# Result quarters in buffers of their own, the global rows' stores on two queues, and their first product earlier in line

## The chip, the cores and the metric

The kernel runs on one core of a Trainium2 chip. The metric is the device time of one execution in microseconds (us), median of the runs. The core has five engines that run their own instruction streams in order and wait for each other by semaphores: PE (TensorE, matrix products; PEld is its weight load), DVE (VectorE), ACT (ScalarE), POOL (GpSimd) and SP (SyncE, which here only issues transfers). In the profile an engine's name with a q (SPq, DVEq) is its sequencer: issuing a DMA and waiting stand there.

## The reference

```python
# attention: B, H, Sl, Sg, D = 8, 8, 512, 32, 64; keys and values are [global; local]
s_g = scale * q_g @ k_all.T                       # 32 global rows see all 544
out_g = softmax(s_g) @ v_all
s_l = scale * [q_l @ k_g.T, masked(q_l @ k_l.T)]  # 512 local rows see 32 global rows and a band of +-32
out_l = softmax(s_l) @ [v_g; v_l]
x = [out_g; out_l] of every batch, heads side by side: (8 * 544, 512)
# feed-forward
h = x @ w_in                                      # 512 -> 2048
g = h * clip(h + 3, 0, 6) / 6
out = g @ w_out                                   # 2048 -> 512, float32, (4352, 512)
```

## The kernel before, in words

All work is done for one batch after another. For each batch b the attention of four groups of 128 local rows and of the 32 global rows is worked out, its result is turned into `xt[b % 3]`, and then the feed-forward of the 512 local rows follows (`ffn_local`). The global rows of all eight batches, 8 x 32 = 256 rows, are gathered in `xg` and go through the feed-forward together at the very end (`ffn_global`); in the code that is "batch 8".

**First product** ("M1", `first`, L1000): for each of 16 chunks c of the 2048 hidden columns PE multiplies four times (L1007) into one PSUM bank, ACT makes the clipped factor (L1013, tile `t1`), and DVE multiplies the two (L1017) into `gl`, which frees the bank. For local rows a multiplication is 512 columns wide, for the global rows 256.

**Second product.** Batches 6, 7 and 8 (`SEVEN`, L998) do it by a scheme with seven products instead of eight. `sevenths` (L1082) has DVE or POOL add and subtract chunks of `gl` into `vs` (L1070); `pair` (L1099) then multiplies, for 256 rows at a time, seven times, each a run of 8 multiplications 128x256 (`product`, L1123), named by m = 0 to 6 here. Sums of these products are kept in two float32 scratch tiles `ub` (in `xt` and `qT`, taken in turn by the pairs; a pair copies its first product there, L1175, and adds to it, `plus`, L1134). Each pair ends in four quarters of its result, 128 rows x 256 columns: `outs` (L1138) has DVE add a bank and a scratch tile into a staging buffer (L1147), and SP stores that buffer to the output. Batch 6 has two pairs, batch 7 two and batch 8 (the global rows) one, so there are 20 quarters.

**Staging and stores.** Before the change the staging buffer is one of three `ot` tiles (`NOT`, L315), shared with the other batches' results. A quarter takes one (`take=("ot",)`) and the store gives it back, so DVE must not write it again until the store from it has landed. A local quarter is one store of 128 rows x 1 KB (L1214). The rows of a global quarter lie in four batches, so it is four stores of 32 rows (L1240). All are issued by SP, one after another.

**Order of work.** The order on every engine is not written out by hand: each operation is entered with an estimated cost, its predecessors and a rank (`Plan.add`), `Plan.run` plays it through with these costs, and the engines get the order that results (L1373). `pick` (L1326) chooses PE's next operation; among the feed-forward's it takes the one with the lowest `key` (L1288). A batch has 32 pieces of key (`PIECES`); for the global rows M1 had the keys 256 + 0 to 15, and the second product 256 + 16 and up. Batch 7's second product has keys 256 + 1 and up (two per product), so the global rows' M1 and batch 7's second product are interleaved.

With these, PE's order from the first global M1 on is, before the change (P7.0 and P7.1 are the two pairs of batch 7, P8 that of batch 8; in brackets m):

```
7 M1, P7.0[1], 1 M1, P7.0[2], 1 M1, P7.0[3], 2 M1, P7.0[4], 2 M1, P7.0[5], 2 M1, P7.0[6], 1 M1,
P7.1[0], P8[0], P7.1[1], P8[1], P7.1[2], P8[2], P7.1[3], P8[3],
P7.1[4], P8[4], P7.1[5], P8[5], P7.1[6], P8[6]
```

Of the kernel before, what the change touches and what calls it, by code (L numbers as in the profile page):

```python
# [10 lines left out]
FP32 = mybir.dt.float32  # L11
# [228 lines left out]
def kernel(  # L240
# [12 lines left out]
    nc = tc.nc  # L253
    P = 128

    B, H, Sl, D = q_l.shape
    Sg = q_g.shape[2]
# [3 lines left out]
    NJ = Sl // P  # L261
    NU = Sl // Sg
    UJ = P // Sg
    NDFF = dff // P
# [33 lines left out]
    vn = sbs("vn", 2, [P, NJ + 1, H, D1])  # L298
# [14 lines left out]
    NT1 = 4  # L313
    t1 = sbs("t1", NT1, [P, Sl], FP32)
    NOT = 3  # L315
# [13 lines left out]
    NM = 3  # L329
# [4 lines left out]

    plan = Plan()
    add = plan.add
    plan.free = {"m": NM, "t": 2, "s": 4, "a": 4, "t1": NT1, "ot": NOT}
    slots = {"m": list(range(NM)), "t1": list(range(NT1)), "ot": list(range(NOT))}

    def dma(rows, run):  # L340

# [719 lines left out]
    wt = [t.rearrange("p (c f) -> p c f", c=NH) for t in wt]  # L1061
    ut = [t.bitcast(FP32) for t in (xt[(B - 3) % 3].rearrange("p n c -> p (n c)"), qT[0].rearrange("d j p q -> d (j p q)"))]
    wt_op = [None] * 4
    u_use = {}

    def both(dst, a, b, op, n, engines, deps, rank, what):
# [32 lines left out]
    def pair(b, i, n, g, s_, sums, gates, store, banks):  # L1099
        a1, a2 = slice(i * P, (i + 1) * P), slice(n + i * P, n + (i + 1) * P)  # L1100
        left, right = slice(0, HALF), slice(HALF, dm)
        lo, hi = range(NH), range(NH, NDFF)
        k = u_use.setdefault("n", 0) % 2
        u_use["n"] += 1
        ub = [ut[k][:, e * HALF:(e + 1) * HALF] for e in range(4)]
        st = {}
        g1, g2 = [gates[c] for c in lo], [gates[c] for c in hi]

        where = ({"X": (0, left), "W": (0, right), "Y": (1, left), "V": (1, right)} if banks == 2 else
                 {x: (y, left) for y, x in enumerate("XYWV")})  # L1110
        two = banks == 2

        def at(x):
            return pm[st[where[x][0]]][:, where[x][1]]

        prev = [None]

        def product(m, x, lhs, rhs, deps, take=None):
            def emit():
                if take is not None:  # L1120
                    st[take] = slots["m"].pop(0)
                for c in range(NH):
                    nc.tensor.matmul(out=at(x), lhsT=lhs(c), rhs=rhs(c), start=c == 0, stop=c == NH - 1)  # L1123
            prev[0] = add("PE", (NH * (HALF / 2.4 + 2.6), NH), emit, [prev[0]] + deps, (b, 2 * i, m * 8 / 7.0),
                          take=("m",) if take is not None else (), what="M2" if take is not None else "M2+")
            return prev[0]

        def freed(x):
            if x is not None:
                slots["m"].append(st[x])  # L1130

        def plus(dst, a, x, deps, bank=None):
            def emit():
                nc.vector.tensor_tensor(out=dst, in0=a(), in1=at(x), op=ALU.add)  # L1134
                freed(bank)
            return add("DVE", 410.0, emit, deps, (-2.5,), give=("m",) if bank is not None else (), what="sevenths")

        def outs(row, cols, x, a, deps, bank):  # L1138

            so = {}  # L1140
            give = ("m",) if bank is not None else ()
            op = add("DVE", 400.0, None, deps, (-2.4,), take=("ot",), give=give, what="out")

            def emit():
                so["o"] = slots["ot"].pop(0)
                dst = ot[so["o"]][:, 0:HALF]
                nc.vector.tensor_tensor(out=dst, in0=a, in1=at(x), op=ALU.add)  # L1147
                freed(bank)
            op.emit = emit

            def emit_store():
                store(i, row, cols, ot[so["o"]])
                slots["ot"].append(so["o"])
            add("SP", (660.0, P * 62.0 / 16, 62.0, P), emit_store, [op], (b, 2 * i, 9), DMA_LAT, give=("ot",), what="store")
            return op

        def gt(c0, cols):
            return lambda c: g[:, c0 + c, cols]

        def wo_(c0, cols):  # L1160
            return lambda c: w_out[:, c0 + c, cols]

        def su(k_):
            return lambda c: s_[:, k_, c, a1]

        def wt_(k_):
            return lambda c: wt[k_][:, c, :]

        used = u_use.get(k, [])
        p1 = product(0, "X", gt(0, a1), wo_(0, left), g1 + wo, 0)  # L1170
        cx = add(("ACT", "DVE"), (act(HALF), dve(HALF)), None, [p1] + used + m1_done[B - 3] + [s_op[B - 2][j] for j in range(NJ + 2)], (-2.5,), lat=220.0, what="sevenths")

        def copy_x():
            if cx.on == "ACT":
                nc.scalar.copy(out=ub[0], in_=at("X"))  # L1175
            else:
                nc.vector.tensor_copy(out=ub[0], in_=at("X"))
        cx.emit = copy_x
        p6 = product(1, "Y", su(1), wt_(1), sums[1] + [wt_op[1]], 1)
        u2 = plus(ub[1], lambda: ub[0], "Y", [p6, cx], None if two else 1)  # L1180
        p7 = product(2, "W", su(2), wt_(2), sums[2] + [wt_op[2]] + ([cx] if two else []), None if two else 2)
        u3 = plus(ub[2], lambda: ub[1], "W", [p7, u2])
        p5 = product(3, "V", su(0), wt_(0), sums[0] + [wt_op[0]] + ([u2] if two else []), None if two else 3)
        u4 = plus(ub[3], lambda: ub[1], "V", [p5, u2])
        c22 = outs(1, right, "V", ub[2], [p5, u3], None)
        p2 = product(4, "X", gt(NH, a1), wo_(NH, left), g2 + [cx] + ([u3] if two else []))
        c11 = outs(0, left, "X", ub[0], [p2], None if two else 0)
        p3 = product(5, "V", su(3), wo_(NH, right), sums[3] + [c22, u4])
        c12 = outs(0, right, "V", ub[3], [p3, u4], 1 if two else 3)
        p4 = product(6, "W", gt(NH, a2), wt_(3), [u3, wt_op[3]] + ([c11] if two else []))  # L1190
        c21 = outs(1, left, "W", ub[2], [p4], 0 if two else 2)
        u_use[k] = [c11, c12, c21, c22]
        m2_done[b].append(p4)

    def ffn_local(b):
        x = xt[b % 3]
        r = b % 2
        parts = ((0, 2), (2, 4)) if b == 0 else ((0, 4),)
        gates = {}
        for part, (j0, j1) in enumerate(parts):  # L1200
            t0, n = j0 * P, (j1 - j0) * P
            for c in range(NDFF):
                free = m2_done[b - 2] if b >= 2 else vperm[0] + vperm[1] if b == 1 else []
                deps = x_op[b][j0:j1] + wi[c // (NDFF // 4)]

                place = 2 * (c % NH) + c // NH if b in SEVEN else c
                pe, ga = first(lambda m, t0=t0, n=n: x[:, m, t0:t0 + n], n, g_l[r][c][:, t0:t0 + n], c, deps,
                               (b, part, place), "M1", free)
                m1_done[b].append(pe)
                gates[part, c] = ga  # L1210
        if b in SEVEN:
            def quarter(i, row, cols, o):
                r0 = b * S + Sg + (2 * row + i) * P
                nc.sync.dma_start(out=out[r0:r0 + P, cols], in_=o[:, 0:HALF])  # L1214
            sevenths(b, g_all[r], Sl // 2, [gates[0, c] for c in range(NDFF)], vs[r], [], quarter, SEVEN[b])
            return
        for j in range(NJ):
            row = b * S + Sg + j * P
            part = next(k for k, (j0, j1) in enumerate(parts) if j0 <= j < j1)


            half = dm // 2
            for i, cols in enumerate((slice(0, half), slice(half, dm)) if (b, j) == (B - 1, NJ - 1) else (slice(0, dm),)):
                def store(o, row=row, cols=cols):
                    nc.sync.dma_start(out=out[row:row + P, cols], in_=o[:, 0:cols.stop - cols.start])
                m2_done[b].append(second(g_l[r], j * P, [gates[part, c] for c in range(NDFF)], (b, j + i), store, "M2", cols))

    def ffn_global():
# [6 lines left out]
        per = P // Sg  # L1235
        rows = out.rearrange("(b s) d -> b s d", s=S)
        if B in SEVEN:
            def quarter(i, row, cols, o):
                for a in range(per):
                    nc.sync.dma_start(out=rows[row * per + a, 0:Sg, cols], in_=o[a * Sg:(a + 1) * Sg, 0:HALF])  # L1240
            sevenths(B, g_all[B % 2], B * Sg // 2, gates, vs[B % 2], m2_done[B - 2], quarter, SEVEN[B])
            return
        for i in range(B // per):
# [35 lines left out]
    EARLY = 40000  # L1279
    KEYS = (47, 44, -23, 52, 0)  # L1280
    REST = 0

    SOONER = (0, 0, 0, 0, 0, 0, 0, 0)
    KEYED, GLAST = 0, 0
# [3 lines left out]
    def key(op):  # L1288
        if op.key is None:
# [2 lines left out]
                op.key = -1e9  # L1292
            elif r[0] == B:

                op.key = B * PIECES + (r[2] if w == "M1" else NDFF + 4 * r[1] + r[2])
            elif w == "M1":
                op.key = r[0] * PIECES + 2.0 * (r[2] + r[1] * 0.5)
            elif w[0] == "M":
# [109 lines left out]
```

## Time and profile before

| | |
|---|---|
| three runs | 331.44, 332.47, 332.88 us; median 332.47 |
| the profiled execution | 332.08 us |
| its span, first to last instruction | 330.3 us, so 1.78 us lie around the span |
| granted TensorE clock | 0.998 of full speed |

A page of the profile gives busy times by engine; the timeline gives each instruction's start and duration, counted from the span's start, with the idle time before it and what ended that; the view of one source line gives the spread of its durations; the chain of waits goes back from the last instruction to what released each step. A store has two times: its issue on the queue of the engine that issues it (SPq rows), and its landing after that, which the view of the line gives as "DMA to landing".

### The profile page before, as it was taken

The page shows a single profiled execution, that of the slowest core. Times are in us where ns is not written, and L with a number is a line of the kernel's source. Part 1 is how long each engine was busy: PE and PEld are TensorE (multiplying, and loading weights), DVE is VectorE, ACT ScalarE, POOL GpSimd, SP SyncE. Part 2 cuts the span into 40 slices and gives each one's busy share as a digit, 9 for nine tenths or more (in the row PEclk, how much of TensorE's full clock was granted, in tenths as well). Part 3 has the DMA queues.
Part 4 walks back from the last instruction along what each step waited for, and adds up shares of the span by engine and source line. Part 5 has one row for each costly group of instructions (what it writes and reads, how often), then busy time and mean ns, then how long its engine had stood idle before and what let it go on. Part 6 is the DMA issues. An engine that isn't in the chain of part 4 may idle for free.

```text
span 330.3 us, 12995 instructions
## 1 busy us (share of the span) xinstructions
PE 313.9 (95%) x5176; PEld 175.0 (53%) x5176; DVE 264.4 (80%) x1038; ACT 226.8 (69%) x553; POOL 225.4 (68%) x322
## 2 busy tenths in 40 slices
PE   7999888999999899999999999998999999999991
PEld 3446666555444445454445444444444456668881
DVE  3799998677987589959985987599978988879742
ACT  4699998779986797489967966657668645335400
POOL 8487544797399959979978998799970640646300
PEclk9999999999999999999999999999999999999999
DMA  8999999998399999699979998993067512210213
GB/s 129 223 202 188 195 237 194 146 151 186 45 151 182 182 189 115 113 147 147 184 125 146 150 133 156 133 169 81 16 151 118 116 36 69 72 33 33 66 34 93
DMA packets 101212, 43.24 MB, mean 131 GB/s; under 512 B 75968, under 2 KB 98080, under 8 KB 101152
## 3 DMA queue, kind: packets, MB, share of 16 engines
q0 software_dynamic: 45840, 17.47, 47.4%
q1 hardware_dynamic: 55312, 24.95, 38.5%
q8 instruction: 40, 0.66, 0.9%
q14 instruction: 20, 0.16, 0.2%
HBM read 35.13 MB, written 8.91 MB: 133 GB/s over the span
## 4 chain that ended last, share of the span: by engine, by line
PE 71%; DVE 18%; issue 4%; DMA 2%; ACT 2%; SPq 1%; POOL 1%; DVEq 0%; ACTq 0%; POOLq 0%
PE m L1033 22%; PE m L1007 22%; DVE gl L1017 5%; PE m L1123 4%; DVE vs L647 4%; DVE sm L833 3%; PE a L864 3%; PE t L1007 3%; PE s L821 3%; DMA kn<-in_k_l_dram 2%; PE s L1007 2%; PE s L1123 2%; PE t L850 1%; ACT t L1013 1%; PE t L1033 1%
## 5 line engine op out<-in xcount | busy, mean ns | idle before, releaser
L647 POOL COPY vs<-vn 32x528 f16<-32x528 f16 (+1 forms) x186 | 115.8, 622 | 19.3 <-ACT vn L383 5.2
L1007 PE MATMUL m<-xt,win 128*128 128x512 f16 (+1 forms) x496 | 105.1, 352 | 2.6 <-DVE gl L1017 2.4
L837 ACT ACTIVATE ex<-sm,mx 128x128 f16<-128x128 f32 x256 | 85.2, 397 | 19.1 <-DVE mx L833 18.4
L1033 PE MATMUL m<-wout,gl 128*128 128x512 f16 x368 | 90.5, 380 | 0.2 <-DVE gl L1017 0.2
L1017 DVE SCALAR_TENSOR_TENSOR gl<-t,m 128x512 f16<-128x512 f32 (+1 forms) x130 | 76.8, 604 | 16.0 <-ACT t L1013 14.6
L1013 ACT ACTIVATE t<-m 128x512 f32<-128x512 f32 (+1 forms) x130 | 68.5, 539 | 30.5 <-PE m L1007 27.2
L1007 PEld LDWEIGHTS <-win 128*128 128x128 f16 x640 | 59.6, 98 | 51.1 <-issue 4.1
L833 DVE CUSTOM_DVE_ANT_0 sm<-s,mask 128x128 f32<-128x128 f32 x256 | 59.7, 285 | 12.4 <-PE s L821 11.2
L1033 PEld LDWEIGHTS <-gl 128*128 128x128 f16 x384 | 34.5, 98 | 38.5 <-issue 0.6
L1070 POOL TENSOR_TENSOR vs<-gl 128x512 f16<-128x512 f16 (+1 forms) x12 | 12.0, 998 | 33.6 <-DVE gl L1017 24.2
L878 DVE TENSOR_TENSOR x<-a,rec 128x256 f16<-128x256 f32 x64 | 24.0, 417 | 0.1
L355 POOL DMA_DIRECT2D vn<-in_v_l_dram x24 | 21.1, 882 | 1.2 <-DMA kn<-in_k_l_dram 0.8
L833 DVE DVE_READ_ACCUMULATOR2_ANT mx<- 128x1 f32 x256 | 21.3, 83 | 0.0
L821 PE MATMUL s<-kT,qT 64*32 64x128 f16 x1024 | 14.2, 219 | 3.6 <-issue 2.0
L1123 PEld LDWEIGHTS <-vs 128*128 128x128 f16 x160 | 15.7, 98 | 3.5
L821 PEld LDWEIGHTS <-qT 64*32 64x32 f16 x1024 | 8.1, 91 | 14.9 <-issue 14.4
L355 POOL DMA_DIRECT2D vn<-in_v_g_dram x7 | 4.1, 584 | 17.4 <-PE a L967 16.9
L383 ACT COPY et<-t 128x1024 f16<-128x1024 f16 (+1 forms) x13 | 12.8, 987 | 4.5 <-PE t L850 4.5
L864 PEld LDWEIGHTS <-et 128*32 128x32 f16 x1024 | 10.1, 96 | 10.3 <-issue 8.1
L647 DVE COPY vs<-vn 64x528 f16<-64x528 f16 (+1 forms) x24 | 14.2, 591 | 0.6
L864 PE MATMUL a<-vs,et 128*32 128x65 f16 x1024 | 14.3, 195 | 0.2 <-DVE vs L647 0.2
L1007 PE MATMUL t<-xt,win 128*128 128x512 f16 x56 | 14.4, 379 | 0.0
(160 smaller groups left out, 436.7 us busy)
## 6 DMA issues: line engine op xcount, KB each, us to landing
out_dram<-ot SPq DMA_DIRECT2D x24, 256.0 KB, 3.6
qn<-in_q_l_dram POOLq DMA_DIRECT2D x16, 256.0 KB, 5.6
kn<-in_k_l_dram POOLq DMA_DIRECT2D x16, 256.0 KB, 6.9
vs<-vn SPq DMA_DIRECT2D x14, 264.0 KB, 5.9
vn<-in_v_l_dram POOLq DMA_DIRECT2D x24, 128.0 KB, 5.2
win<-in_moe_w_in_dram POOLq DMA_DIRECT2D x4, 512.0 KB, 9.1
wout<-in_moe_w_out_dram POOLq DMA_DIRECT2D x8, 256.0 KB, 9.4
out_dram<-ot SPq DMA_DIRECT2D x16, 128.0 KB, 1.7
```

Of the source, the lines that this page charges most:

```text
L355: op = add("POOL", dma(rows, run), lambda: nc.gpsimd.dma_start(out=dst, in_=src), deps, rank, LOAD_LAT + (MARGIN if what[0] in "vqkg" and ...
L647: (nc.vector if o.on == "DVE" else nc.gpsimd).tensor_copy(out=dst, in_=src)
L821: nc.tensor.matmul(out=pss[e][u * Sg:(u + 1) * Sg, p * P:(p + 1) * P], lhsT=qT[r][rows, j, p, u * Sg:(u + 1) * Sg], rhs=kT[r][rows, p, k0: ...
L833: nc.vector.tensor_tensor_reduce(out=sm[i3][h], in0=pss[e][:, p * P:(p + 1) * P], in1=m, scale=-scale, scalar=3.0e38, op0=ALU.add, op1=ALU ...
L837: nc.scalar.activation(out=ex[ie][:, h, :], in_=sm[i3][h], func=EXP, scale=-1.0, bias=mx[i3][h])
L864: nc.tensor.matmul(out=psa[h // 4][q, c0:c0 + D + 1], lhsT=et[k][:, h * P + u * Sg:h * P + (u + 1) * Sg], rhs=vs[r][:, j * UJ + u, h, 0:D ...
L878: nc.vector.tensor_tensor(out=xs[ix][:, 4 * c * D:4 * (c + 1) * D].rearrange("q (h d) -> q h d", d=D), in0=acc[c][:, :, 0:D], in1=rr[c].to ...
L1007: nc.tensor.matmul(out=ps[:, 0:n], lhsT=w_in[:, m, c * P:(c + 1) * P], rhs=x(m), start=(m == 0), stop=(m == NP - 1))
L1013: nc.scalar.activation(out=t1[st["t"]][:, 0:n], in_=pm[st["m"]][:, 0:n], func=RELU, bias=0.5, scale=1.0 / 6.0)
L1017: nc.vector.scalar_tensor_tensor(out=g, in0=t1[st["t"]][:, 0:n], scalar=1.0, in1=pm[st["m"]][:, 0:n], op0=ALU.min, op1=ALU.mult)
L1033: nc.tensor.matmul(out=pm[st["m"]][:, 0:n], lhsT=g[c][:, t0:t0 + P], rhs=w_out[:, c, cols], start=(c == 0), stop=(c == NDFF - 1))
L1123: nc.tensor.matmul(out=at(x), lhsT=lhs(c), rhs=rhs(c), start=c == 0, stop=c == NH - 1)
```

## The change

- The quarters of batches 6, 7 and 8 get five staging buffers of their own (`oq`), which lie in `vn[0]`, the value tile of the even batches. A quarter therefore also waits for the attention of batch 6, which last reads that tile.
- Of a global quarter's four stores, ACT's queue issues the first two and SP's the last two.
- The planner's costs of a store are other numbers.
- The keys of the global rows' M1 go up by 0.5 instead of 1, and those of their second product begin at 12 instead of 16 (`GLOBALS`).

```diff
-    plan.free = {"m": NM, "t": 2, "s": 4, "a": 4, "t1": NT1, "ot": NOT}
-    slots = {"m": list(range(NM)), "t1": list(range(NT1)), "ot": list(range(NOT))}
+    plan.free = {"m": NM, "t": 2, "s": 4, "a": 4, "t1": NT1, "ot": NOT, "oq": 5}
+    slots = {"m": list(range(NM)), "t1": list(range(NT1)), "ot": list(range(NOT)), "oq": list(range(5))}
...
+    oq = vn[0].rearrange("p n h d -> p (n h d)")[:, 0:10 * HALF].bitcast(FP32).rearrange("p (k c) -> p k c", k=5)
...
-            op = add("DVE", 400.0, None, deps, (-2.4,), take=("ot",), give=give, what="out")
+            op = add("DVE", 400.0, None, deps + [av_op[B - 2][j] for j in range(NJ + 1)] + strips[B - 2], (-2.4,), take=("oq",), give=give, what="out")
 
             def emit():
-                so["o"] = slots["ot"].pop(0)
-                dst = ot[so["o"]][:, 0:HALF]
+                so["o"] = slots["oq"].pop(0)
+                dst = oq[:, so["o"], :]
                 nc.vector.tensor_tensor(out=dst, in0=a, in1=at(x), op=ALU.add)
                 freed(bank)
             op.emit = emit
 
+            half = [add("ACT", 900.0, lambda: store(i, row, cols, oq[:, so["o"], :], nc.scalar), [op], (-1,), lat=0.0, what="store")] if b == B else []
+
             def emit_store():
-                store(i, row, cols, ot[so["o"]])
-                slots["ot"].append(so["o"])
-            add("SP", (660.0, P * 62.0 / 16, 62.0, P), emit_store, [op], (b, 2 * i, 9), DMA_LAT, give=("ot",), what="store")
+                store(i, row, cols, oq[:, so["o"], :], nc.sync)
+                slots["oq"].append(so["o"])
+            add("SP", (900.0 if b == B else 450.0, P * 62.0 / 16, 62.0, P), emit_store, [op] + half, (b, 2 * i, 9), DMA_LAT, give=("oq",),
+                what="store")
...
-            def quarter(i, row, cols, o):
+            def quarter(i, row, cols, o, queue):
                 r0 = b * S + Sg + (2 * row + i) * P
-                nc.sync.dma_start(out=out[r0:r0 + P, cols], in_=o[:, 0:HALF])
+                queue.dma_start(out=out[r0:r0 + P, cols], in_=o)
...
-            def quarter(i, row, cols, o):
-                for a in range(per):
-                    nc.sync.dma_start(out=rows[row * per + a, 0:Sg, cols], in_=o[a * Sg:(a + 1) * Sg, 0:HALF])
+            def quarter(i, row, cols, o, queue):
+
+                for a in range(per // 2) if queue is nc.scalar else range(per // 2, per):
+                    queue.dma_start(out=rows[row * per + a, 0:Sg, cols], in_=o[a * Sg:(a + 1) * Sg, :])
...
+    GLOBALS = (0, 0.5, 12)
...
-                op.key = B * PIECES + (r[2] if w == "M1" else NDFF + 4 * r[1] + r[2])
+                op.key = B * PIECES + (GLOBALS[0] + GLOBALS[1] * r[2] if w == "M1" else GLOBALS[2] + 4 * r[1] + r[2])
```

All engines' orders are the same in both kernels up to the last 31 us, but for the staging buffers. From the first global M1 on, PE's order after the change is:

```
7 M1, P7.0[1], 5 M1, P7.0[2], 4 M1, P7.0[3],
P7.1[0], P7.0[4], P8[0], P7.0[5], P8[1], P7.0[6], P8[2], P7.1[1], P8[3], P7.1[2], P8[4],
P7.1[3], P8[5], P7.1[4], P8[6], P7.1[5], P7.1[6]
```

The last quarters of the result stand in DVE's order after the change as: global, global, local, global, local, global, local, local. SP issues for them: global (2 stores), global (2), local, local, global (2), local, global (2), local; ACT issues the eight others after its last computing instruction. One of the 16 sums of the global rows goes from DVE to POOL.

## The prediction

> **What bounds the kernel now.** I read three views in this order: busy time by stretch of the span, to find the stretch in which PE stops being the bound; the timeline of that stretch; and the stores' two lines, for the price of an issue and a landing. The stretches first (columns: length, then busy us and instructions of PE, PEld, DVE, ACT, POOL; then granted clock, the DMA engines' mean busy share, GB/s):
>
> ```profile
> core 0: us, PE busy (x) PEld busy (x) DVE busy (x) ACT busy (x) POOL busy (x), PEclk, DMA share, GB/s
> 299.20:312.20 13.00, 13.00 (x122) 11.65 (x120) 11.77 (x29) 6.52 (x17) 8.61 (x11) 1.00 0.13 42
> 312.20:318.40 6.20, 6.20 (x60) 5.55 (x58) 3.44 (x10) 0.75 (x2) 0.00 (x0) 1.00 0.07 22
> 318.40:323.60 5.20, 5.20 (x49) 4.50 (x46) 2.44 (x6) 0.00 (x0) 0.00 (x0) 1.00 0.31 94
> 323.60:330.30 6.70, 0.09 (x1) 0.00 (x0) 0.84 (x2) 0.00 (x0) 0.00 (x0) 0.88 0.28 83
> ```
>
> PE is busy without a gap until 323.6 and then has nothing left, yet the span goes on for 6.7 us. In that time DVE works 0.84 us, ACT and POOL nothing, and the DMA engines are 28% busy. So neither arithmetic nor bandwidth fills these 6.7 us. The timeline of the end shows what does:
>
> ```profile
> 319.26 1.74 SPq L1240 DMA_DIRECT2D out_dram<-ot  x4
> ...
> 321.10 0.37 SPq L1214 DMA_DIRECT2D out_dram<-ot  x1
> 321.56 1.77 SPq L1240 DMA_DIRECT2D out_dram<-ot  x4
> ...
> 322.26 0.42 DVE L1147 TENSOR_TENSOR ot<-qT,a 128x256 f32<-128x256 f32 x1 [1.61 <-DMA out_dram<-ot]
> 322.65 1.04 PE L1123 MATMUL m<-kn,gl 128*128 128x256 f16 x8
> 322.95 0.42 DVE L1147 TENSOR_TENSOR ot<-xt,s 128x256 f32<-128x256 f32 x1 [0.27 <-DMA out_dram<-ot]
> 323.43 0.37 SPq L1214 DMA_DIRECT2D out_dram<-ot  x1
> 323.89 1.77 SPq L1240 DMA_DIRECT2D out_dram<-ot  x4
> 324.76 0.42 DVE L1147 TENSOR_TENSOR ot<-qT,s 128x256 f32<-128x256 f32 x1 [1.39 <-DMA out_dram<-ot]
> 325.29 0.42 DVE L1147 TENSOR_TENSOR ot<-xt,m 128x256 f32<-128x256 f32 x1
> 325.76 0.37 SPq L1214 DMA_DIRECT2D out_dram<-ot  x1
> 326.23 1.77 SPq L1240 DMA_DIRECT2D out_dram<-ot  x4
> ```
>
> From 319.26 to 328.00 (326.23 + 1.77) SP's queue issues store after store with pauses of at most 0.1 us. DVE waits three times (1.61, 0.27, 1.39 us) for a staging buffer, because the store that empties it stands in that queue. The last product ends at 323.69 (322.65 + 1.04), but the last of its stores is issued only at 327.6. The price of one store, from the views of the two store lines and one link of the chain of waits:
>
> ```profile
> L1240 SPq DMA_DIRECT2D out_dram<-ot x16: 344/412/421, 319.3 to 327.6; - x16
> DMA to landing us min/median/max: 1.5/1.6/1.6
> L1214 SPq DMA_DIRECT2D out_dram<-ot x4: 333/368/368, 318.4 to 325.8; - x4
> DMA to landing us min/median/max: 1.7/1.7/1.7
> 322.91 1.56 DMA out_dram<-ot
> ```
>
> A small store takes 0.41 us of queue and follows its predecessor after 0.46 (four take 1.77); a local one takes 0.37. The link of the chain starts where the fourth issue of its group starts (321.56 + 3 x 0.45), so landing counts from an issue's start: a small store lands 1.56 - 0.41 = 1.15 us after its issue ends, a local one 1.7 - 0.37 = 1.33. Check on the end: 328.00 + 1.15 = 329.15, and 1.15 us of closing waits give the span of 330.3. **The bound of the last 10 us is SP's issue**: in that stretch PE makes a local and a global quarter every two products, 2 x 0.87 = 1.74 us, while their five issues cost 0.46 + 4 x 0.46 = 2.3 us.
>
> **The change, part by part.**
>
> *Half of the global stores on ACT's queue.* SP's share of such a pair falls to 0.46 + 2 x 0.46 = 1.4 us, below PE's 1.74. SP no longer falls behind. The trace has no ACT-issued transfer, so its price c is unknown. ACT has no other work by then:
>
> ```profile
> 313.24 0.37 ACT L1175 COPY xt<-m 128x256 f32<-128x256 f32 x1 [0.50 <-PE m L1123]
> L361 SPq DMA_DIRECT2D gl<-in_q_g_dram x1: 384/384/384, 0.7 to 0.7; - x1
> L355 POOL DMA_DIRECT2D vn<-in_v_l_dram x24 | 21.1, 882 | 1.2 <-DMA kn<-in_k_l_dram 0.8 <-DMA qn<-in_q_l_dram 0.4
> ```
>
> Before, ACT's last instruction is the copy at 313.24; after, it is the same copy for the global pair, near 312. So nothing of ACT's own work stands in front of the stores, and behind a store that waits for its quarter stand only ACT's later stores. The nearest rows for c are SP's 0.34 to 0.42, and from above POOL's 0.88. A queue's first use shows no surcharge on SP (its first transfer, 0.384). I take 0.41, the row for the very same transfer. Half of the transfers can't cost less than nothing, and c below 0.41 gains nothing, since the last store is SP's. How far c may rise: the first global quarter is ready at about 317.5 (worked out below), and eight issues in a row end at 317.5 + 8(c + 0.05); with 1.15 for the landing that passes the forecast's last landing, 326.4, only when c exceeds 0.9. POOL's price would cost some tenths at most.
>
> The DMA engines' share of 0.31 above shows that the transfers leave room; whether two queues can issue at once no row shows. The Trainium skill, "Perfetto Trace Analysis", section "DMA Instruction — HWDGE (DVE, Sync)", speaks against it: the block that generates descriptors is shared by the issuing sequencers and locked for exclusive use. It doesn't say how much of an issue falls under the lock. By that rule, with whole issues under it, the time would be that of rival 1 below, 330.8; without it, the sum's.
>
> *Five buffers instead of three.* With two queues a global quarter holds its buffer for 0.42 (DVE) + 0.87 (two issues) + 1.15 (landing) + 0.3 (from landing, 322.91 + 1.56 = 324.47, to DVE's start at 324.76) = 2.75 us. Near the end one buffer is wanted per product, every 0.87 us. Three come round after 2.6 us and would cost up to 0.15 us per turn, some 0.4 us over the last eight quarters; five come round after 4.35 and cost nothing. Alone, without the second queue, the buffers would gain about 0.1: SP has no pause to give back. The new condition, that batch 6's attention has read `vn[0]`, costs nothing:
>
> ```profile
> L967 PE MATMUL a<-vn,et x80: 191/193/206, 249.4 to 285.0; 128*32 128x65 f16 x80
> 279.11 0.41 DVE L1147 TENSOR_TENSOR ot<-xt,m 128x256 f32<-128x256 f32 x1
> ```
>
> These 80 are the global rows' value products of batches 6 and 7: the 40 at 249.4 read `vn[0]`, those at 284.8 `vn[1]`; the first quarter is written at 279.11, 30 us after the last reading.
>
> *The global M1 sooner.* (The planner's new store costs act only through this order.) PE has the same products before and after, so its sum stays: 323.69. What moves is what they need. Two rows of the chain give the price of an M1 and of a product, one gives the last M1 before:
>
> ```profile
> 299.23 0.44 PE m L1007 x4
> 302.29 0.87 PE m L1123 x8
> 311.02 0.44 PE s L1007 x4
> 312.37 0.29 DVE L1070 TENSOR_TENSOR vs<-gl 128x256 f16<-128x256 f16 x1
> 313.02 0.29 DVE L1070 TENSOR_TENSOR vs<-gl,vs 128x256 f16<-128x256 f16 x1
> 309.19 0.55 DVE L1070 TENSOR_TENSOR vs<-gl 128x256 f16<-128x256 f16 x1
> 309.67 0.67 POOL L1070 TENSOR_TENSOR vs<-vs,gl 128x256 f16<-128x256 f16 x1
> ```
>
> (The rows at 312.37 and 313.02 are the first and last of three sums.) After, the M1 end at 299.2 + 16 x 0.44 + 2 x 0.87 = 308.0 instead of 311.46. The first product on the last sums is P8[1], behind P7.0[3], P7.1[0], P7.0[4], P8[0] and P7.0[5]: 308.0 + 5 x 0.87 = 312.3. Before, the last sum ended 1.85 us after the last M1 (313.31 less 311.46), which would now be 309.9. But DVE has its work closer together: by 312.3 it must have done the 11.77 us of its first stretch, plus these three sums (0.87), less three quarters that now come later (3 x 0.42) and the one sum that goes to POOL (0.3): 11.1 us from 299.2 on, so done at 310.3, or at 311.5 if it keeps the 1.2 us that it idled in that stretch. That is 0.8 to 2 us of cover. The far end: 311.5 with those three sums slowed beside POOL's (0.55 each, the row at 309.19, so 0.8 more) and one POOL sum (0.67) waited for in full is 312.9, a stall of 0.6 us. The near end is no gain, since PE has no pause to lose. I take no stall. Beyond the cover this part gains nothing by itself: had a global quarter stayed last, two issues on each queue would end 0.92 us after DVE, and the order after ends no sooner.
>
> **The sum.** Near 317.5 the first global quarter is written: P8[3] is the tenth product after the last M1 and ends at 308.0 + 10 x 0.87 = 316.7, then `plus` and the quarter take 0.8 us. From there SP has 8 x 0.46 + 4 x 0.42 = 5.4 us of issues for 6.7 us of PE and DVE. At the end: last product 323.69; quarter 323.74 to 324.15; by then SP is still busy, since the next to last quarter (DVE until 323.28, one product of 0.87 earlier) is issued at 323.32 to 323.69 and the last global one, which stands behind it, takes 2 x 0.46 to 324.65. The last store is issued from 324.69 to 325.06, lands at 326.39, and with 1.15 of closing waits the span is 327.54: **2.76 us less**. The profiled execution took 332.08, so **329.3 us**. That execution lies 0.4 below the median of the three runs (332.47; 331.44 to 332.88), a scatter that the range must hold as well. A measurement of this kernel can tell about 0.5%, 1.7 us, from no change; 2.76 is 0.8%.
>
> **The rivals.**
>
> 1. *SP's and ACT's issues take turns*, one transfer description at a time, instead of running beside each other. No row here has two such queues at work. Twenty issues from 317.5 on, 16 x 0.46 + 4 x 0.42 = 9.0, end at 326.5; with 1.33 and 1.15 the span is 329.0, and the time 330.8. For it: nothing in the trace excludes it. Against it: the DMA engines are only 28 to 31% busy, so the data at least need not take turns.
> 2. *DVE falls behind the packed M1* and PE stalls by the far end of 0.6 us, near P8[1] or P7.0[5]: 329.9. Against: the cover above.
> 3. *ACT's issue is dear.* The dearest issue of any queue here is below; at that c = 1.12 the eight end at 317.5 + 9.4 = 326.9 and land at 328.0, span 329.2: 331.0. Against: it is a transpose, another kind of transfer.
>
> ```profile
> 287.24 1.12 SPq L365 DMA_TRANSPOSE xg<-xgn  x1
> ```
>
> 4. *The other side: ACT's eight stores last longer than the queue they relieve.* Same place; beyond 10.5 us for the eight with any first-use cost (328.0 less 317.5) the kernel is slower than before, by over 0.5% from 12.2 us on, 1.5 us each; at c = 1.6 the time is 317.5 + 13.2 + 1.15 + 1.15 + 1.78 = 334.8. Against it: no issue in the trace costs that.
>
> That the change doesn't do what it says is excluded where it could be: ACT's stores stand behind no computation.
>
> **How the numbers follow.** Forecast 0.64 (329.3; 328.8 if SP's last backlog of 0.5 vanishes; the scatter of the runs on either side), stall 0.08 (329.9), turns 0.14 (330.8), dear issue 0.07 (331.0), slower 0.07. Faster by over 0.5% (below 330.4): forecast and stall, 0.72. Within 0.5%: turns and nearly all of the dear issue, 0.20. Slower: 0.08. The range reaches from 328.3 (the lower bound less 0.5 of scatter) to 331.2, which takes in rivals 1 to 3 and leaves rival 4 out.
>
> **What would show it.** Right: PE without gaps from 299.2 to 323.7; ACTq rows of about 0.41 us that begin near 317.5 and lie beside SPq rows; no DVE quarter idle on a DMA; the last SPq store near 324.7; some 3.9 us instead of 6.7 behind the last product. Wrong: ACTq or SPq issues of 0.8 to 0.9 where both queues work (rival 1); PE idle on DVE before P7.0[5] or P8[1] (rival 2); ACTq rows over 0.9 with SPq rows unchanged (3, 4); quarters that wait for a store of the other queue.

## The result and the profile after

| | before | after |
|---|---|---|
| median of five runs | 331.77 us (331.12 to 332.88) | 329.51 us (329.03 to 330.08) |
| ratio, 95% interval | | 0.9927 (0.9901 to 0.9952) |
| profiled execution | 332.08 us | 329.03 us |
| its span | 330.3 us | 327.2 us |
| first global M1 begins (a row of the timeline) | 299.07 us | 298.70 us |
| tail: from there to the span's end | 31.23 us | 28.50 us |

The runs say 0.7% faster; the forecast was 0.8%. The ratios leave out runs more than 1.5% above the fastest of their kernel (two of the ten of `e_bufs` below). For the single parts I use the **tail**. The place where it begins wanders from profile to profile by more than the effect (297.29 to 300.29 us over all kernels of this study, whose orders are the same up to there), while the tail repeats: a second profile of the changed kernel gave 28.51. That is the only repeat: every other tail below is from one profile, and as a span is given to 0.1 us, a tail is good to about 0.05.

The stretches of after, in the columns of the prediction's first view:

```profile
299.20:312.20 13.00, 13.00 (x121) 11.65 (x120) 11.54 (x30) 6.95 (x19) 8.90 (x12) 1.00 0.10 32
312.20:318.40 6.20, 6.20 (x59) 5.54 (x58) 3.28 (x9) 0.00 (x0) 0.00 (x0) 1.00 0.17 55
323.32:327.20 3.88, 0.00 (x0) 0.00 (x0) 0.42 (x1) 0.00 (x0) 0.00 (x0) 0.97 0.30 93
```

PE is still without a gap until its last product ends at 323.32, and behind it lie 3.88 us instead of 6.61 (330.3 less 323.69; forecast: 3.9). The end of the timeline shows where the rest went (start, duration, then engine and instruction):

```profile
317.15 2.19 SPq L1246 DMA_DIRECT2D out_dram<-vn  x4
317.15 5.80 ACTq L1246 DMA_DIRECT2D out_dram<-vn  x8
...
319.77 1.76 SPq L1219 DMA_DIRECT2D out_dram<-vn  x2
...
321.58 0.94 SPq L1246 DMA_DIRECT2D out_dram<-vn  x2
321.61 0.42 DVE L1149 TENSOR_TENSOR vn<-xt,a 128x256 f32<-128x256 f32 x1 [0.45 <-DMA out_dram<-vn]
...
322.28 1.04 PE L1125 MATMUL m<-kn,gl 128*128 128x256 f16 x8
322.48 0.42 DVE L1149 TENSOR_TENSOR vn<-qT,s 128x256 f32<-128x256 f32 x1 [0.45 <-PE s L1125]
322.93 0.35 SPq L1219 DMA_DIRECT2D out_dram<-vn  x1
323.32 0.92 SPq L1246 DMA_DIRECT2D out_dram<-vn  x2
323.35 0.42 DVE L1149 TENSOR_TENSOR vn<-qT,m 128x256 f32<-128x256 f32 x1 [0.45 <-PE m L1125]
324.34 0.37 SPq L1219 DMA_DIRECT2D out_dram<-vn  x1
```

Before, SP's queue was full to 328.00; now it has pauses (319.34 to 319.77, for one), and its last store is issued at 324.34. DVE's quarters follow PE again, one per 0.87 us. The row at 321.61 still names a DMA, but is no wait for one: the product that it reads ended at 321.57 (a row at 320.53 with 1.04), and every quarter here idles the same 0.45 us for PE. What is left of SP's queue at the end is a backlog: the last quarter is written at 323.77, but two stores of the last global quarter, written by 322.03, hold SP until 324.24.

The second queue, from the views of the two store lines:

```profile
L1246 SPq DMA_DIRECT2D out_dram<-vn x8: 314/414/468, 317.1 to 323.8; - x8
L1246 ACTq DMA_DIRECT2D out_dram<-vn x8: 321/420/467, 317.2 to 322.5; - x8
DMA to landing us min/median/max: 1.5/1.6/1.7
L1219 SPq DMA_DIRECT2D out_dram<-vn x4: 350/352/367, 319.8 to 324.3; - x4
DMA to landing us min/median/max: 1.7/1.7/1.7
```

An ACT issue takes 0.42 us, an SP issue of the same transfer 0.41, as before. Both queues begin at 317.15. The two issues that begin side by side there, from the view of the same line between 317.1 and 317.5, then two more between 318.5 and 318.6, and one of ACT's that begins alone at 320.3:

```profile
L1246 SPq DMA_DIRECT2D out_dram<-vn x1: 345/345/345, 317.1 to 317.1; - x1
L1246 ACTq DMA_DIRECT2D out_dram<-vn x1: 407/407/407, 317.2 to 317.2; - x1
L1246 SPq DMA_DIRECT2D out_dram<-vn x1: 314/314/314, 318.6 to 318.6; - x1
L1246 ACTq DMA_DIRECT2D out_dram<-vn x1: 375/375/375, 318.6 to 318.6; - x1
L1246 ACTq DMA_DIRECT2D out_dram<-vn x1: 321/321/321, 320.3 to 320.3; - x1
```

Neither waits for a whole issue of the other. ACT's takes 0.05 to 0.06 us longer beside SP's (0.375 at 318.6, 0.380 at 322.1) than alone (0.321), and no issue of the line takes over 0.468.

### The profile page after: what moved, and what is told of

Same layout as the page of the kernel before. It is cut to its first block, busy times and chain, and to the rows that moved or that the text cites. A ratio compares the mean times of both kernels' runs of the same rounds, so it can differ in the third digit from the quotient of the medians.

```text
span 327.2 us, 12991 instructions
## 1 busy us (share of the span) xinstructions
PE 314.4 (96%) x5176; PEld 174.8 (53%) x5176; DVE 264.2 (81%) x1037; ACT 226.5 (69%) x553; POOL 226.1 (69%) x323
## 4 chain that ended last, share of the span: by engine, by line
PE 71%; DVE 14%; DMA 4%; POOL 4%; issue 3%; ACT 2%; ACTq 0%; POOLq 0%
PE m L1033 22%; PE m L1007 21%; PE m L1125 5%; DVE gl L1017 5%; PE a L864 3%; PE t L1007 3%; PE s L821 3%; DVE vs L647 2%; DVE sm L833 2%; PE s L1125 2%; DMA win<-in_moe_w_in_dram 2%; DMA kn<-in_k_l_dram 2%; PE s L1007 2%; POOL vs L647 2%; PE a L1007 1%
## 5 line engine op out<-in xcount | busy, mean ns | idle before, releaser
L1072 POOL TENSOR_TENSOR vs<-gl 128x512 f16<-128x512 f16 (+1 forms) x13 | 12.7, 977 | 31.3 <-DVE gl L1017 21.9
```

## The experiments

Each is told by its tail. In the expectations after's tail stands as 28.39; its first M1 was read there from a row that begins at 298.81 and lacks the first multiplication, and 28.50 is right. The three parts of the change, each in or out, give eight kernels; before and after are two of them, the other six follow. The planner's costs of a store go with the queue: the old ones with SP alone, the new ones with two queues. Each ratio is against the runs of before in its own session.

| queues | buffers | order | kernel | tail, us | less than before | times against before (95%) |
|---|---|---|---|---|---|---|
| SP | 3 | old | before | 31.23 | | |
| SP | 5 | old | e_bufs | 31.27 | -0.04 | 1.0002 (0.9979 to 1.0024) |
| SP | 3 | new | e_keys | 30.21 | 1.02 | 0.9963 (0.9941 to 0.9985) |
| SP | 5 | new | e_bufs_keys | 30.25 | 0.98 | 0.9975 (0.9951 to 1.0000) |
| SP, ACT | 3 | old | e_split | 29.10 | 2.13 | 0.9929 (0.9902 to 0.9956) |
| SP, ACT | 3 | new | e_split_keys | 28.79 | 2.44 | 0.9910 (0.9885 to 0.9935) |
| SP, ACT | 5 | old | e_split_bufs | 28.77 | 2.46 | 0.9936 (0.9901 to 0.9972) |
| SP, ACT | 5 | new | after | 28.50 | 2.73 | 0.9927 (0.9901 to 0.9952) |

In all eight PE's last product begins 23.58 us after the first global M1: what differs lies behind PE alone. The theory was that SP's issue set the end; the main rival, that DVE's waits for a staging buffer did, which the profile shows as 3.3 us.

**Five buffers alone.**

The diff is against after (L1153, L1158, L1245, L1288; `...` marks what is left out):

```diff
-            half = [add("ACT", 900.0, lambda: store(i, row, cols, oq[:, so["o"], :], nc.scalar), [op], (-1,), lat=0.0, what="store")] if b == B else []
+            half = [add("ACT", 900.0, lambda: store(i, row, cols, oq[:, so["o"], :], nc.scalar), [op], (-1,), lat=0.0, what="store")] if False else []
...
-            add("SP", (900.0 if b == B else 450.0, P * 62.0 / 16, 62.0, P), emit_store, [op] + half, (b, 2 * i, 9), DMA_LAT, give=("oq",),
+            add("SP", (660.0, P * 62.0 / 16, 62.0, P), emit_store, [op] + half, (b, 2 * i, 9), DMA_LAT, give=("oq",),
...
-                for a in range(per // 2) if queue is nc.scalar else range(per // 2, per):
+                for a in range(per):
...
-    GLOBALS = (0, 0.5, 12)
+    GLOBALS = (0, 1, 16)
```

> One part alone: five staging buffers of their own; all stores on SP and the old order of M1. Theory (SP's issue was the bound): DVE's waits for a buffer vanish, but SP has no pause to give back, so its queue ends at the same time: tail 31.2 as before, within 0.15. Rival (staging buffers were the bound): DVE writes the last quarter near 324.2 on the scale of before instead of 325.7, and the tail is 1.5 to 2.8 us shorter, 28.4 to 29.7.

Measured: 31.27. The end of its timeline:

```profile
322.48 0.42 DVE L1149 TENSOR_TENSOR vn<-xt,m 128x256 f32<-128x256 f32 x1 [0.45 <-PE m L1125]
322.66 1.77 SPq L1246 DMA_DIRECT2D out_dram<-vn  x4
324.53 0.37 SPq L1219 DMA_DIRECT2D out_dram<-vn  x1
325.00 1.76 SPq L1246 DMA_DIRECT2D out_dram<-vn  x4
```

No quarter waits for a buffer any more; DVE writes the last one 24.65 us after the first M1 (322.48 less 297.83) where before it was 26.22 (325.29 less 299.07). And the kernel ends at the same time: the finished quarter lies there for 2.1 us until SP comes to it. The waits were shown in the profile and were real, but they were the queue's shadow: the end that they seemed to delay was set by the queue anyway. The rival falls.

**The second queue alone.**

Against after, with the stores reading the same slice of `ot` and the buffers' bookkeeping back to before's (both left out here):

```diff
-                so["o"] = slots["oq"].pop(0)
-                dst = oq[:, so["o"], :]
+                so["o"] = slots["ot"].pop(0)
+                dst = ot[so["o"]][:, 0:HALF]
...
-    GLOBALS = (0, 0.5, 12)
+    GLOBALS = (0, 1, 16)
```

> One part alone: half of each global quarter's stores on ACT's queue; three staging buffers and the old order of M1. Measured by the tail, from the first global M1 to the span's end: 31.23 us before (299.07 to 330.3), 28.39 after (298.81 to 327.2). Theory (SP's issue was the bound): SP's cost of a local and a global quarter falls from 2.3 to 1.4 us, below PE's 1.74, so nearly the whole gain comes: tail 28.9 (2.3 less than before), the rest lost to a last global quarter and to waits of some tenths for three buffers. Rival (staging buffers were the bound: DVE waited 3.27 us for them): the three buffers stay, so the waits stay, tail 30.5 to 31.2.

Measured: 29.10, 2.13 less than before (2.3 expected). The waits stay, as rows of this kind:

```profile
321.53 0.42 DVE L1149 TENSOR_TENSOR ot<-qT,a 128x256 f32<-128x256 f32 x1 [1.45 <-DMA out_dram<-ot]
323.82 0.42 DVE L1149 TENSOR_TENSOR ot<-xt,m 128x256 f32<-128x256 f32 x1 [0.50 <-DMA out_dram<-ot]
```

Four of them sum to 2.5 us, and yet they cost 0.33 (29.10 less 28.77 with five buffers): a waiting quarter holds up only its own store, and PE does not wait for it (its last product begins at the same 23.58 us).

**The order alone.**

Against before, whose three buffers and single queue stay (L1295 of before; the lines that only pass the queue and the slice along are left out):

```diff
+    GLOBALS = (0, 0.5, 12)
-                op.key = B * PIECES + (r[2] if w == "M1" else NDFF + 4 * r[1] + r[2])
+                op.key = B * PIECES + (GLOBALS[0] + GLOBALS[1] * r[2] if w == "M1" else GLOBALS[2] + 4 * r[1] + r[2])
```

> One part alone: the global rows' M1 sooner in line; all stores on SP, three buffers. Theory (SP's issue was the bound): the first global quarter is ready about 1.3 us sooner (the tenth product after the last M1, near 317.5 on the scale of before, instead of a first store of four at 319.26 behind a local one at 318.39), and SP's 20 issues of 9.0 us follow each other from there: tail 29.9, 1.3 less. The prediction took this part alone as worth nothing, but only beside the second queue. Rival (the order matters only through a local quarter as the last one): 4 x 0.46 less 0.37, tail 29.7 with SP's queue idle in between; rival (it does nothing): 31.2.

Measured: 30.21, 1.02 less, 0.3 short of the 29.9. The prediction's sentence that this part gains nothing by itself does not hold where SP's queue is the bound: there it lets the 20 issues begin sooner. The rival "nothing" (31.2) is out. The other rival gave 29.7 and asked for pauses of SP; the rows show none of more than 0.11 us from 318.74 on:

```profile
318.74 3.59 SPq L1246 DMA_DIRECT2D out_dram<-ot  x8
322.43 0.37 SPq L1219 DMA_DIRECT2D out_dram<-ot  x1
322.89 1.77 SPq L1246 DMA_DIRECT2D out_dram<-ot  x4
324.77 0.37 SPq L1219 DMA_DIRECT2D out_dram<-ot  x1
325.23 1.77 SPq L1246 DMA_DIRECT2D out_dram<-ot  x4
327.10 0.84 SPq L1219 DMA_DIRECT2D out_dram<-ot  x2
```

That is the whole queue: its 20 issues take 9.20 us, from 18.45 after the first M1 (318.74 less 300.29) to 27.65 (327.94), where I had reckoned 9.0 (0.46 from one issue to the next holds for the local ones too, not 0.42). With the landing and the closing 27.65 + 1.33 + 1.15 = 30.13 of the 30.21.

**Without the new order, without the buffers, without the second queue.** Each is after with one part undone.

> The change without its third part: two queues and five buffers, but the old order of M1, with a global quarter last. Theory as the prediction had it (the order gains nothing beside the second queue: two issues on each queue after the last quarter end 0.92 us after DVE, as SP's backlog does in the order after): tail 28.4 to 28.8. Rival (the order is worth 1 us or more also beside the second queue, as without it): tail 29.4 or more.

Measured: 28.77. So the order is worth 0.27 beside the other two, not nothing. Its last rows show why:

```profile
323.36 0.35 SPq L1219 DMA_DIRECT2D out_dram<-vn  x1
323.75 1.87 SPq L1246 DMA_DIRECT2D out_dram<-vn  x4
323.78 0.42 DVE L1149 TENSOR_TENSOR vn<-xt,m 128x256 f32<-128x256 f32 x1 [0.45 <-PE m L1125]
```

I had counted two issues after the last quarter; but SP comes to them with a backlog here too (two stores of the global quarter before, in the same row x4) and ends 26.49 us after the first M1 instead of 26.01. Of these 0.48 some 0.18 come back, as a small store lands 1.15 us after its issue ends and a local one 1.33.

> The change without the buffers: two queues and the new order, three staging buffers. Theory: a global quarter holds its buffer 2.75 us, three come round after 2.6, so DVE waits some 0.15 to 0.4 us per turn from 320 on; these show as idle time of the quarters behind a DMA, but PE has two products of room before it needs the bank: tail 28.5 to 28.9. Rival (buffers were the bound): tail 30 or more.

Measured: 28.79, as expected. But the profile names a DMA for no quarter's wait, and only the quarter at 320.48 begins later than its product lets it, by some 0.14 us. With three buffers the planner put the last global quarter (the row `ot<-xt,a`) behind the two local ones, and its two stores end SP's queue:

```profile
322.96 0.42 DVE L1149 TENSOR_TENSOR ot<-qT,m 128x256 f32<-128x256 f32 x1 [0.45 <-PE m L1125]
323.30 0.41 DVE L1149 TENSOR_TENSOR ot<-xt,a 128x256 f32<-128x256 f32 x1
323.83 0.86 SPq L1246 DMA_DIRECT2D out_dram<-ot  x2
```

SP ends 26.38 us after the first M1 (324.69 less 298.31) instead of 26.01. So most of the 0.29 is paid in order and not in the waits that were expected.

> The change without the second queue: five buffers and the new order, all stores on SP. Theory (SP's issue is the bound): SP's 20 issues of 9.0 us follow each other from the first global quarter: tail 29.9, as with the order alone, so the second queue is worth 1.5 us beside the other two. Rival (buffers were the bound, the queue is not): as after, 28.4 to 28.6.

Measured: 30.25, 0.35 over the 29.9: the 20 issues take 9.2 us here too. The second queue is worth 1.75 beside the other two (1.5 expected).

**A price of ACT's stores twice and four times as high.** Each of ACT's stores is cut into two of 32 rows x 128 columns (x2), or four of 16 x 128 (x4, where the pair `(1, 2)` below is `(2, 2)`).

```diff
-                    queue.dma_start(out=rows[row * per + a, 0:Sg, cols], in_=o[a * Sg:(a + 1) * Sg, :])
+                    nr, nc_ = (1, 2) if queue is nc.scalar else (1, 1)
+                    for x in range(nr):
+                        for y in range(nc_):
+                            rs, cs, w = Sg // nr, HALF // nc_, cols.start
+                            queue.dma_start(out=rows[row * per + a, x * rs:(x + 1) * rs, w + y * cs:w + (y + 1) * cs],
+                                            in_=o[a * Sg + x * rs:a * Sg + (x + 1) * rs, y * cs:(y + 1) * cs])
```

> After, with the suspected price doubled: each of ACT's eight stores cut into two of 32 rows x 128 columns, so that a store of the change costs ACT about 0.9 us of queue. Tail of after 28.5 (two profiles: 28.50 and 28.51). Theory by the prediction's bound (ACT's price begins to set the end only above 0.9 us a store): sixteen issues of 0.46 from 18.45 us after the first M1 end at 25.8, before SP's last at 26.0, tail 28.5, within 0.2. Rival (the two queues take turns at the descriptors): sixteen ACT issues beside SP's twelve no longer fit, tail 29.5 or more; SPq or ACTq issues of over 0.6 us.

> After, with the suspected price four times as high: each of ACT's eight stores cut into four of 16 rows x 128 columns, about 1.8 us of queue for what was 0.42. This is the prediction's fourth rival made real: slower than before once the eight last over 10.5 us. Theory: 32 issues of 0.46 = 14.7 us from 18.45 us after the first M1 end at 33.2, with 1.15 and 1.15 the tail is 35.5, 4.3 us over before's 31.23, and DVE's last quarters wait for buffers. Rival (a queue's issues of small stores are cheaper, 0.3 or less, and the price isn't per store): tail under 31.

Measured: x2 28.91, 0.4 more than after, where at most 0.2 was expected; x4 35.70 (35.5 expected), ratio to before 1.0143 (1.0090 to 1.0197). The rows of x4:

```profile
L1250 ACTq DMA_DIRECT2D out_dram<-vn x32: 353/431/442, 316.3 to 331.0; - x32
316.35 15.04 ACTq L1250 DMA_DIRECT2D out_dram<-vn  x32
324.97 0.42 DVE L1149 TENSOR_TENSOR vn<-qT,s 128x256 f32<-128x256 f32 x1 [3.16 <-DMA out_dram<-vn]
```

A quarter of the bytes costs the same 0.43 us: the price is per store. So the kernel does become slower once the second queue lasts longer than what it relieves; the prediction's fourth rival had the right mechanism and price, at a c that no single issue here has. The rival of turns falls with x2: it asked for 29.5 or more and for issues of over 0.6 us, and the longest of either queue's small stores takes 0.443. For x2 ACT's issues end 25.99 us after the first M1, as reckoned (25.8), and SP's at 26.01, where after has 26.01 too. So the 0.4 lie behind the last issue. The views of the last store of each queue in x2:

```profile
L1219 SPq DMA_DIRECT2D out_dram<-vn x1: 370/370/370, 322.9 to 322.9; - x1
DMA to landing us min/median/max: 2.1/2.1/2.1
L1250 ACTq DMA_DIRECT2D out_dram<-vn x1: 432/432/432, 322.8 to 322.8; - x1
DMA to landing us min/median/max: 1.8/1.8/1.8
```

SP's last store lands 2.1 us after its issue began, where all four of its kind in after took 1.7: 322.93 + 2.1 + 1.15 = 326.18 of a span of 326.2. ACT's last lands before it, at 324.65 (322.85 + 1.8). So the 0.4 is the later landing of SP's last store. What makes it late was not tried, and stays open.

**All four stores of the last global quarter on ACT.** In after ACT ends at 322.95, SP at 324.71, with the backlog named above. (`row == 1` and `cols.start == 0` pick the last global quarter out.)

```diff
-for a in range(per // 2) if queue is nc.scalar else range(per // 2, per):
+own = per if row == 1 and cols.start == 0 else per // 2
+for a in range(own) if queue is nc.scalar else range(own, per):
```

> After, with all four stores of the last global quarter on ACT's queue. Theory: SP's backlog of 0.5 us in front of the last local store (issued at 324.34 in the trace of after, while its quarter is written at 323.77) goes, ACT's four end before that: tail 27.9, 0.45 to 0.5 less than after. Rival (the end is set by something else behind the last quarter): 28.4. Rival (the two queues get in each other's way): four ACT issues of over 0.6 us would end last, 28.4 or more.

> The changed kernel once more, beside the version with the last global quarter on ACT: tail 28.4 again, within 0.15; the upstream part before the first global M1 may differ by some tenths from run to run.

Measured: 27.99 against 28.51 for after in the same session, 0.52 less, just over the 0.45 to 0.5 that were expected. The last store follows its quarter directly:

```profile
322.54 1.23 SPq L1219 DMA_DIRECT2D out_dram<-vn  x2
322.97 0.42 DVE L1149 TENSOR_TENSOR vn<-qT,m 128x256 f32<-128x256 f32 x1 [0.45 <-PE m L1125]
```

By the tail this version is the shortest. The medians are 328.11 us for it, 328.43 for after and 331.18 for before; the ratios to before 0.9905 (0.9881 to 0.9930) for it and 0.9917 (0.9889 to 0.9944) for after. Those two intervals overlap nearly whole, so the runs alone don't separate it from after.

## Why the prediction was right

- **What bounds the end.** SP's issue, not DVE's waits and not PE. `e_bufs` shows that it isn't the waits (gone, same end), the PE row at 23.58 us in all eight kernels that it isn't PE; `e_split` (2.13 less by the second queue alone), `e_last_act` (SP's backlog gone, 0.52 less) and x4 (slower once ACT's queue ends last) show the queues.
- **ACT's price, 0.41 us with no surcharge for the first.** Measured 0.42, the first one 0.407. That first one is not quite free of a surcharge: in `e_split_bufs`, where ACT's first issue begins alone, it takes 0.391, and ACT's lone issue at 320.3 in after 0.321; 0.07 us is too little to matter here. The nearest row of another queue was the right one. That the trace held nothing of ACT made the range wide, not the value wrong.
- **The two queues beside each other.** The rule of the Trainium skill, "Perfetto Trace Analysis", section "DMA Instruction — HWDGE (DVE, Sync)", that the descriptor generator is shared and locked, would have given 330.8 if whole issues fell under the lock. This case's trace differs from that reading: the two queues' first issues begin within 0.1 us of each other and take 0.345 and 0.407 us. If there is a lock, it holds a small part of an issue: beside one of SP's, ACT's issue grows by 0.05 to 0.06 us, and the longest issue with two queues is 0.477 (`e_split_bufs`) against 0.421 before. Left open is why SP's small store right behind a local one takes 0.468 and 0.451 in after against 0.373 to 0.378 before; no issue of ACT's begins with it.
- **The sum.** Forecast: tail 28.47 (327.54 less 299.07); measured 28.50 and 28.51. It came out this near because the end is a short chain with one row each, and each came as reckoned: counted from the first M1, the last quarter is written at 25.07 (forecast 25.08), the last issue ends at 26.01 (25.99), it lands at 27.34 (27.32).
- **The order's part.** Wrong by 0.3 us: "Beyond the cover this part gains nothing by itself: had a global quarter stayed last, two issues on each queue would end 0.92 us after DVE". The runs show a gain of 0.27 beside the two other parts and 1.02 alone. The failing step compared the two orders' last quarters but gave the backlog in front of it only to the new order.
- **The cover for PE.** PE did not stall. The rows of after that decide it, the last sum and the product that needs it:

```profile
310.15 0.29 DVE L1072 TENSOR_TENSOR vs<-gl,vs 128x256 f16<-128x256 f16 x1
311.80 1.04 PE L1125 MATMUL a<-qn,vs 128*128 128x256 f16 x8
```

  1.36 us lie between (311.80 less 310.44); the forecast was 0.8 to 2.
- **The buffers' part.** 0.4 us forecast for three buffers beside two queues; 0.33 measured with the old order, 0.29 with the new one, where it is paid in another way. For the buffers alone 0.1 was forecast, and -0.04 measured, no difference that a tail can show.
- **The size by runs.** 2.26 us by the medians, 3.05 by the two profiled executions, 2.73 by the tails. The difference between the last two comes from where the tail begins (0.37 us earlier in after), which the change has no part in: the orders are the same up to there. Without it the profiled 329.03 would be 329.40, beside the forecast of 329.3.

## What to carry to other kernels

Find the queue that has no pause before the last landing; waits that ended with a transfer from that queue were its shadow here, and removing them alone gave nothing. Many small stores at the end were paid by the store and not by the byte, on the queue that issued them. A second queue that was idle by then took eight of 20 issues (3.7 us) and brought the end 2.1 us forward by itself; behind that PE's pace set the rest. With its issues at four times their number (x4) it ended last, and the kernel was slower than before. For effects of 1% measure the stretch that changes, from a fixed instruction to the end, and not only the whole.

## What the runs showed of the hardware

- Issuing a store of 32 rows x 256 columns costs 0.42 us of ACT's queue and 0.41 of SP's, one of 16 x 128 0.43 of ACT's. A quarter of the bytes saves nothing.
- Two queues issue beside each other: ACT's issue took 0.375 to 0.380 us where one of SP's began with it, 0.321 alone, and SP's beside it no more than alone (0.314 and 0.345 against 0.344).
- A store that is the same in two kernels can land later in one: SP's last local store landed 1.7 us after its issue began in after, 2.1 in x2.
